# First layer of batches 1 to 3 in two levels of the seven-product scheme, with block sums on GpSimd

## The chip, the cores and the metric

The kernel runs on one core of one Trainium2 chip. The metric is the device time of one execution in microseconds, all work included, from one launch. Lower is better. The core has five engines with queues of their own: PE (matrix products, with PEld for the load of the stationary operand), DVE, ACT, POOL (GpSimd) and SP, which only issues transfers here.

## What is computed

Attention with a bucket mask for 4 batches of 8 heads of 768 x 64, then a Fourier mix, a normalisation and a two-layer network. Cut to what matters:

```python
# q, k, v: (4, 8, 768, 64); proj: (64, 6)
mask = bucket(q @ proj)[..., :, None] == bucket(k @ proj)[..., None, :]
attn = softmax(where(mask, q @ k.T / 8, -1e9))
x = heads_side_by_side(attn @ v)                      # (4, 768, 512)

mixed = real(fft(fft(x, axis=1), axis=2))
u = x + mixed
un = (u - mean(u)) / sqrt(var(u) + 1e-6)
out = u + maximum(un @ w_ch1, 0) @ w_ch2              # w_ch1: 512 x 2048, w_ch2: 2048 x 512
```

All products are in float32. The change is in `un @ w_ch1`, the first layer.

## The kernel before, in words

**Stages.** After the attention of all batches, each batch goes through `mix(b)`: the Fourier products (lines 1071 and 1100), with DVE adding the results to x (line 1114), and then `mlp7(b)`, the two layers. The 2048 rows of the first layer's output are worked in two halves: first layer half 0, second layer half 0 (`outer7`), first layer half 1, second layer half 1. The second layer's matmuls are at line 1275, the first layer's at line 1394.

**Seven products.** Both layers use Winograd's form of Strassen's scheme: a product of two matrices cut in 2 x 2 blocks is made of seven block products instead of eight, with sums of blocks ahead of and behind them. In the first layer the weights are the left matrix, 16 block rows of 128; for each of eight pairs of block rows `f` (four in a half) there are seven products (`A11, S2, A12, S1, S3, S4, A22`), each of two matmuls, 128 x 128 on 128 x 384. The left sums are made once, in batch 0, by `quarters(f)` (line 1181), and are written to DRAM (`ad`, lines 1193 and 1194). Batches 1 to 3 read the left blocks back through a ring of 12 slots of 128 KB that lies where the weights w1 were (`fetch`, line 1367, on SP's queue); one block is fetched for each product. The right sums (t1 to t4 of 768 columns, lines 1372 to 1379) are made of x by DVE at the start of the batch.

**Evictions.** ACT copies a product from PSUM, DVE adds the copies in SBUF, ACT applies relu (lines 1434 to 1463). The result `hall` has four blocks c11, c12, c21, c22, each 4 x 384 columns in a half.

**Around it.** `across` (line 1121) turns x by PE (four transposes a tile of 128 rows, line 1126), and ACT copies the result out for the second layer; in batches 1 to 3 three of six tiles are turned ahead of the products and three after the first `f`. `spread` (line 1129) makes each row's scale, with two operations on POOL (lines 1136, 1137). `fold(b + 1)` (line 959) is DVE work for the next batch. In batch 0 `weights2` (line 1213) brings the second layer's weights, fetched on POOL's queue (line 714) and converted by ACT and DVE in turn with the first layer; its sums end at line 1244. `store` sends results from POOL's queue (line 947; SP's in the last batch). In the mix POOL sets a few columns of F to zero (line 1062).

**The range test.** `guard` (line 1487) reads q and k again in 32 pieces of 384 KB and lets ACT sum their squares, in turn with batches 1 and 2. It has three slots (`nq`) and fetches two pieces ahead from POOL's queue (line 1497); the square is at line 1508.

**Order.** In this part of the kernel the code gives an order by its generators, and instructions of each engine can be moved ahead of others where their operands allow; `in_turn` and `issue_after` hold some of them behind named instructions. On the chip each queue is then worked strictly in its order.

Of the kernel before, what the change touches and what calls it, by code (L numbers as in the profile page):

```python
# [20 lines left out]
P = 128  # L21
# [462 lines left out]
def _main(  # L484
# [39 lines left out]
    def pt(shape, name):  # L524
        return banks[0](shape, name)
# [639 lines left out]
    ]  # L1165
    at = NR * 2 * P
# [7 lines left out]
    side = [w1f[:, at + i * HALF : at + (i + 1) * HALF] for i in range(2)]  # L1174
# [163 lines left out]
    def mlp7(b):  # L1338
# [6 lines left out]
        ut, sd, ss = [*us], side, s1s  # L1345
        if b == 0:
# [10 lines left out]
            sd = [s1s[0].rearrange("p r n -> p (r n)")[:, 0:HALF]] * 2  # L1357
            ss = [s1s[0], spare[3].rearrange("p (r n) -> p r n", n=P)]
        prods = [A11, S2, A12, S1, S3, S4, A22]
        right = {A11: b11, S2: t2, A12: b21, S1: t1, S3: t3, S4: b22, A22: t4}  # L1360
        todo = [(f, i) for f in range(HF) for i in prods]
        fetched = [0]

        def fetch():
            n = fetched[0]
            if b and n < len(todo):
                nc.sync.dma_start(ring[n % NR], ad[todo[n][0], todo[n][1]])
                fetched[0] += 1

        for _ in range(NR):  # L1370
            fetch()
        nc.vector.tensor_tensor(t1, b12, b11, op=ALU.subtract)
        nc.vector.tensor_tensor(t2, b22, t1, op=ALU.subtract)
        nc.vector.tensor_tensor(t4, b21, t2, op=ALU.subtract)
# [3 lines left out]
        rs = {}  # L1378
        nc.vector.tensor_tensor(t3, b22, b12, op=ALU.subtract)
        hall = late.tile([P, 2, HF // 2, S], F32, tag="F", name=f"h{b}")  # L1380
        done = [0]

        def product(i, ps, start=True):
            n = done[0]
            left = ring[n % NR]
            if b == 0:
                f = n // 7
                if i >= S2:
                    left = qs[:, f % 2, i - S2].rearrange("p (k m) -> p k m", m=P)
                else:  # L1390
                    c, r = (0 if i == A11 else 2), (f + HF if i == A22 else f)
                    left = w1[:, c : c + 2, r * P : (r + 1) * P]
# [6 lines left out]
            fetch()  # L1399
# [3 lines left out]
        def relu(h):  # L1403

            if b == 0:
                held.append(h)
            else:
                done_by[ET.Activation] = nc.scalar.activation(h, h, AF.Relu)  # L1408

        def behind_copy(ins):  # L1410

            if ins is not None and b == 0:
                done_by[ET.Activation] = ins
# [5 lines left out]
        def inner(half):  # L1419
            for r in range(HF // 2):  # L1420
# [28 lines left out]
                nc.scalar.copy(sd[0], p7)  # L1449
                nc.vector.tensor_tensor(c22, c22, sd[0], op=ALU.add)  # L1450
# [10 lines left out]
                behind_copy(nc.scalar.copy(sd[1], p7))  # L1461
                done_by[ET.DVE] = nc.vector.tensor_tensor(c21, c21, sd[1], op=ALU.add)
                relu(c21)
                if b == 0 and f < HF - 1:
                    quarters(f + 1)
# [4 lines left out]

        for half in range(2):
# [8 lines left out]
            for _ in outer7(b, half, hall, ut, rs, ss):  # L1480
                next(ahead, None)
                yield
            for _ in ahead:
                pass


    def guard():

        nq = {}

        def fetch(i):
            if i < 2 * NPAIR * B:
                n, io = divmod(i, 2)
                b, t = divmod(n, NPAIR)
                tl = late.tile([P, S], F32, tag="nq", name=f"nq{i}", bufs=3)
                s = (k if io else q)[b, 2 * t : 2 * t + 2].rearrange("h s d -> (h s d)")
                nc.gpsimd.dma_start(tl, s.rearrange("(p c) -> p c", p=P))
                nq[i] = tl

        with in_turn():  # L1500
            fetch(0)
            fetch(1)
        yield
        for i in range(2 * NPAIR * B):
            with in_turn():
                fetch(i + 2)
                junk = late.tile([P, S], BF16, tag="junk", name=f"junk{i}")
# [97 lines left out]
```

## Time and profile before

| what | us |
|---|---|
| median of 3 runs | 1014.23 |
| lowest, highest | 1014.07, 1014.61 |
| the profiled execution | 1013.47 |
| its span | 1011.7 |

How to read the profile: busy times of PE overlap between instructions, so the rate of matmuls is read from start to start. A matmul of the code in float32 is two records in the trace. In a row of the timeline "x4" means four merged instructions of that kind, and the second number is from the first one's start to the last one's end. In a row of a window the numbers after the length are the busy times of PE, PEld, DVE, ACT and POOL with their instruction counts, the granted clock, the share of the transfer engines and GB/s; a window of one line has only the engines that the line uses.

### The profile page before, as it was taken

The page shows a single profiled execution, that of the slowest core. Times are in us where ns is not written, and L with a number is a line of the kernel's source. Part 1 is how long each engine was busy: PE and PEld are TensorE (multiplying, and loading weights), DVE is VectorE, ACT ScalarE, POOL GpSimd, SP SyncE. Part 2 cuts the span into 40 slices and gives each one's busy share as a digit, 9 for nine tenths or more (in the row PEclk, how much of TensorE's full clock was granted, in tenths as well). Part 3 has the DMA queues.
Part 4 walks back from the last instruction along what each step waited for, and adds up shares of the span by engine and source line. Part 5 has one row for each costly group of instructions (what it writes and reads, how often), then busy time and mean ns, then how long its engine had stood idle before and what let it go on. Part 6 is the DMA issues. An engine that isn't in the chain of part 4 may idle for free.

```text
span 1011.7 us, 14410 instructions
## 1 busy us (share of the span) xinstructions
PE 998.4 (99%) x5169; PEld 651.4 (64%) x5169; DVE 674.0 (67%) x1198; ACT 512.3 (51%) x1029; POOL 87.2 (9%) x179
## 2 busy tenths in 40 slices
PE   8999999999999999999999999999999999999997
PEld 5444444444444766866885785897686689678576
DVE  4788898878986698579979543549553445454353
ACT  5787887878766566066046515234623402531520
POOL 3000000000000101100214100121200020200000
PEclk9999999999999999999999999999999999999999
DMA  9645363554610438036345543154516223314201
GB/s 142 125 90 112 86 160 56 118 98 98 131 41 13 135 105 293 9 99 245 107 170 173 170 161 104 53 198 125 162 58 195 86 87 122 94 53 143 86 21 45
DMA packets 174880, 115.61 MB, mean 114 GB/s; under 512 B 126672, under 2 KB 159952, under 8 KB 174800
## 3 DMA queue, kind: packets, MB, share of 16 engines
q1 hardware_dynamic: 166224, 88.12, 32.4%
q0 software_dynamic: 7008, 26.09, 8.3%
q8 instruction: 43, 0.70, 0.3%
q10 hardware_dynamic: 1568, 0.39, 0.2%
q14 instruction: 37, 0.30, 0.1%
HBM read 93.59 MB, written 20.97 MB: 113 GB/s over the span
## 4 chain that ended last, share of the span: by engine, by line
PE 90%; DVE 5%; ACT 2%; DMA 2%; issue 1%; POOL 1%; SPq 0%; DVEq 0%; ACTq 0%; POOLq 0%
PE o L1275 29%; PE h_p L1394 22%; PE oo L875 13%; PE sc L858 12%; PE sc L848 4%; PE cs L1071 3%; PE A L1100 2%; PE B L1100 2%; PE sum L895 1%; PE bits L812 1%; DMA zraw<-in_moe_w_ch_dram 1%; PE un L1126 1%; DMA kn<-in_k_dram 1%; DVE bs L1132 0%; DMA pjr<-in_proj_dram 0%
## 5 line engine op out<-in xcount | busy, mean ns | idle before, releaser
L1275 PE MATMUL o<-w,h 128*128 128x256 f32 x1152 | 253.9, 379 | 0.0
L1275 PEld LDWEIGHTS o<-w,h 128*128 128x128 f32 x1152 | 219.1, 190 | 30.9
L865 ACT ACTIVATE pk<-sc 128x768 f32<-128x768 f32 x192 | 152.5, 813 | 34.9 <-PE sc L858 31.4
L1394 PE MATMUL h_p<-x,w 128*128 128x384 f32 x448 | 160.7, 488 | 1.9 <-ACT h L1434 1.8
L858 PE MATMUL sc<-qt,kt 64*128 64x384 f32 x768 | 155.6, 482 | 0.0
L875 PE MATMUL oo<-pk,vn 128*64 128x385 f32 (+1 forms) x768 | 134.4, 492 | 0.0
L1394 PEld LDWEIGHTS h_p<-x,w 128*128 128x128 f32 x448 | 84.0, 190 | 60.9 <-ACT h L1434 6.6
L932 DVE TENSOR_TENSOR acc<-acc,pk 128x1536 f32<-128x1536 f32 x63 | 110.1, 1747 | 3.1
L1394 PE MATMUL h_p<-w 128*128 128x384 f32 x288 | 104.8, 486 | 0.0
L875 PEld LDWEIGHTS oo<-pk,vn 128*64 128x64 f32 x768 | 50.9, 136 | 81.0 <-issue 79.2
L858 PEld LDWEIGHTS sc<-qt,kt 64*128 64x128 f32 x768 | 69.5, 188 | 30.5 <-issue 30.0
L1394 PEld LDWEIGHTS h_p<-w 128*128 128x128 f32 x288 | 54.5, 190 | 37.4 <-PE un L1126 0.4
L1287 DVE SCALAR_TENSOR_TENSOR w<-o,rs,w 128x256 f32<-128x256 f32 x56 | 26.9, 481 | 70.4 <-PE o L1275 69.6
L1305 ACT COPY tq<-o 128x256 f32<-128x256 f32 x24 | 8.9, 372 | 105.4 <-PE o L1275 105.4
L1408 ACT ACTIVATE h<-h 128x384 f32<-128x384 f32 x72 | 37.8, 524 | 32.4 <-DVE h L1450 13.4
L848 PEld LDWEIGHTS <-kk 33*128 33x128 bf16 x384 | 19.7, 93 | 50.8 <-issue 28.0
L1294 ACT COPY tq<-o 128x256 f32<-128x256 f32 x24 | 8.9, 369 | 72.0 <-PE o L1275 72.0
L1445 DVE TENSOR_TENSOR h<-h 128x384 f32<-128x384 f32 x32 | 17.8, 556 | 38.2 <-ACT h L1444 38.1
L1275 PE MATMUL o<-w 128*128 128x256 f32 x176 | 41.6, 379 | 0.0
L1321 DVE TENSOR_TENSOR tq<-tq,o 128x256 f32<-128x256 f32 x24 | 10.1, 419 | 40.4 <-PE o L1275 40.4
L1275 PEld LDWEIGHTS o<-w 128*128 128x128 f32 x176 | 33.5, 190 | 4.5
L1438 DVE TENSOR_TENSOR h<-h 128x384 f32<-128x384 f32 x32 | 17.8, 556 | 27.6 <-ACT h L1437 27.4
(162 smaller groups left out, 1370.8 us busy)
## 6 DMA issues: line engine op xcount, KB each, us to landing
w<-ad SPq DMA_DIRECT2D x168, 128.0 KB, 2.1
w<-bd SPq DMA_DIRECT2D x42, 512.0 KB, 4.6
zraw<-in_moe_w_ch_dram SPq DMA_DIRECT2D x16, 512.0 KB, 4.5
zraw<-in_moe_w_ch_dram POOLq DMA_DIRECT2D x16, 512.0 KB, 4.3
bd<-w SPq DMA_DIRECT2D x14, 512.0 KB, 3.5
vn<-in_v_dram SPq DMA_DIRECT2D x32, 192.0 KB, 3.1
nq<-in_q_dram POOLq DMA_DIRECT2D x16, 384.0 KB, 3.7
nq<-in_k_dram POOLq DMA_DIRECT2D x16, 384.0 KB, 3.8
```

Source lines behind the costliest of these rows:

```text
L848: nc.tensor.matmul(pss[g][:, h, 0:HALF], kk[r, ks], bits[1][r] if g else bits[0][r, h], start=start, stop=not start,)
L858: nc.tensor.matmul(pss[g][:, h, 0:HALF], kt[rows, ks], qt[rows, g * HALF : (g + 1) * HALF], start=early, stop=not early,)
L865: nc.scalar.activation(pk[:, g, :, 0:HALF], pss[g][:, :, 0:HALF], AF.Exp, scale=SCALE)
L875: nc.tensor.matmul(oos[g][h * D : (h + 1) * D, 0:w], nat["v", n][:, (2 * c + h) * D : (2 * c + h + 1) * D], pk[:, g, h, 0:w], start=(c == ...
L932: nc.vector.tensor_tensor(acc, (first[:, :, :, 0:HALF] if c == 1 else acc), new, op=ALU.add)
L1071: nc.tensor.matmul(ps[:, pc + 2 * lo : pc + 2 * hi - 1 : 2], z[:, cp, pc, par, t * P : (t + 1) * P], ch[:, cp, pc, lo:hi], start=(cp == 0) ...
L1100: nc.tensor.matmul(ps[:, cols], F[:, par, k, t, j * P : (j + 1) * P], sq[:, t, k, cols], start=(t == 0), stop=(t == 1),)
L1275: nc.tensor.matmul(ps, a[:, r], right7[i][:, r], start=start and r == 0, stop=r == HF // 2 - 1, skip_group_check=not start,)
L1287: nc.vector.scalar_tensor_tensor(t[:, cols], src, r, t[:, cols], op0=ALU.mult, op1=ALU.add)
L1394: nc.tensor.matmul(ps, left[:, k], right[i][:, k], start=start and k == 0, stop=k == 1, skip_group_check=not start,)
L1408: done_by[ET.Activation] = nc.scalar.activation(h, h, AF.Relu)
L1438: done_by[ET.DVE] = nc.vector.tensor_tensor(c21, c12, c21, op=ALU.add)
```

## The change

In batches 1 to 3 each of the seven products of the first layer is itself split into seven. Two block rows of the left side are taken together (`f` and `f + 2` of a half), the right side of 384 columns in two of 192, and each of the 7 x 7 leaf products of a half is two matmuls, 128 x 128 on 128 x 192. That is 98 leaf products a batch where there were 56 products, each still with one left block of 128 KB from DRAM.

- **Left sums.** `blocks2(half)`, run beside batch 0's second layer, reads each of the seven left blocks of a half (512 KB), makes four sums of 512 columns on GpSimd and writes 512 KB to a new DRAM tensor `ad2`, on SP's queue.
- **Right sums.** At the start of a batch `two_levels` makes the four first-level sums on DVE, then `divided` makes four second-level sums of 384 columns for each product: for A11, S2 and A12 on DVE, for S1, S3, A22 and S4 on GpSimd. Some are written over x, so all six tiles of `across` stand ahead of them.
- **Order of leaves.** A product's leaves are seven numbers of a key `7 n + 2 j`, so that two products are interleaved. Each product has four banks.
- **Evictions.** ACT copies two leaves of seven, DVE adds five from PSUM. S4's leaves are added straight onto c12's blocks. Five 1536-column sums a half that join the products (`behind`) are on GpSimd, one on DVE; q0 (the second layer's `tq`) and q1 hold two products each in turn.
- **Range test.** One slot, `side`; the square is written over it, and the next piece is fetched from ACT's queue behind the square.

Batch 0 keeps the one-level form. The loop over the halves is now a function `halves`, which pulls `blocks2` at every second step of batch 0's second layer. The core of the diff:

```diff
+    ad2 = tc.dram_tile([2, 7, 4, P, 2, P], F32, name="ad2")
+    def blocks2(half):
+        rows = slice(half * HF // 2, (half + 1) * HF // 2)
+        both_ = late.tile([P, 2, 2, 8 * P], F32, tag="r2", name=f"blocks{half}")
+        for i in range(7):
+            src = both_[:, i % 2, 0].rearrange("p (f k m) -> p f k m", k=2, m=P)
+            dst = both_[:, i % 2, 1].rearrange("p (s g m) -> p s g m", g=2, m=P)
+            nc.sync.dma_start(src, ad[rows, i].rearrange("f p k m -> p f k m"))
...
+            nc.gpsimd.tensor_tensor(s1, lc, ld, op=ALU.add)
+            nc.gpsimd.tensor_tensor(s2, s1, la, op=ALU.subtract)
+            nc.gpsimd.tensor_tensor(s3, la, lc, op=ALU.subtract)
+            nc.gpsimd.tensor_tensor(s4, lb, s2, op=ALU.subtract)
+            nc.sync.dma_start(ad2[half, i].rearrange("s p g m -> p s g m"), dst)
+            yield
...
-                if b and f == 0:
-                    for T in range(3):
-                        across(b, T, ut[T])
...
-            for _ in outer7(b, half, hall, ut, rs, ss):
+            second = blocks2(half) if b == 0 else iter(())
+            for i, _ in enumerate(outer7(b, half, hall, ut, rs, ss)):
                 next(ahead, None)
+                if i % 2 == 0:
+                    next(second, None)
                 yield
...
+    def two_levels(b, right, hall, ut):
+        order = [A11, S2, A12, S1, S3, A22, S4]
+        leaves = sorted(
+            (half, 7 * n + 2 * j, i, leaf)
+            for half in range(2)
+            for n, i in enumerate(order)
+            for j, leaf in enumerate(range(7))
+        )
...
+        def divided(eng, i):
...
+            for d, x, y in ((t1, rb, ra), (t2, rd, t1), (t4, rc, t2), (rb, rd, rb)):
+                eng.tensor_tensor(d, x, y, op=ALU.subtract)
+            parts[i] = ra, t2, t1, rc, rb, rd, t4
+        for T in range(NT):
+            across(b, T, ut[T])
+        V, G = nc.vector, nc.gpsimd
+        V.tensor_tensor(right[S1], right[S3], right[A11], op=ALU.subtract)
+        V.tensor_tensor(right[S2], right[S4], right[S1], op=ALU.subtract)
+        divided(V, A11)
+        V.tensor_tensor(right[A22], right[A12], right[S2], op=ALU.subtract)
+        V.tensor_tensor(right[S3], right[S4], right[S3], op=ALU.subtract)
+        divided(V, S2)
+        divided(V, A12)
+        for i in (S1, S3, A22, S4):
+            divided(G, i)
...
+        to = {A11: c12, S2: q0, A12: q1, S1: c22, S3: q0, A22: q1}
...
+        def placed(i, j, ps):
+            y = to[i]
+            y00, y01, y10, y11 = (block(y, a, c) for a in range(2) for c in range(2))
+            if j == 0:
+                copy(y01, ps[0])
+            elif j == 1:
+                add(y10, y01, ps[1])
+            elif j == 2:
+                add(y11, y10, ps[2])
+            elif j == 3:
+                copy(y00, ps[0])
+            elif j == 4:
+                add(y11, y11, ps[3])
+            elif j == 5:
+                add(y01, y10, ps[2])
+            else:
+                add(y10, y10, ps[3])
...
+        def behind(i):
+            if i == S2:
+                add(c21, c12, q0, G)
+            elif i == A12:
+                add(c11, c12, q1, G)
+                relu(c11)
+            elif i == S1:
+                add(c12, c21, c22, G)
+            elif i == S3:
+                add(c21, c21, q0)
+                add(c22, c22, c21, G)
+                relu(c22)
+            elif i == A22:
+                for n in range(2):
+                    y, x = (t[:, :, n * HH : (n + 1) * HH] for t in (c21, q1))
+                    add(y, y, x, G)
+                    relu(y)
...
+            at = (0, 1, 2, 0, 3, 2, 3)[j]
+            start = at not in ps
+            if start:
+                ps[at] = pt([P, 2, HH], f"h{b}_{half}_{i}_{at}")
+            for g in range(2):
+                nc.tensor.matmul(
+                    ps[at][:, g], ring[n % NR][:, g], parts[i][j],
+                    start=start and g == 0, stop=g == 1, skip_group_check=True,
+                )
+            fetch()
...
     def guard():
...
-                nc.gpsimd.dma_start(tl, s.rearrange("(p c) -> p c", p=P))
+                nc.scalar.dma_start(side, s.rearrange("(p c) -> p c", p=P))
...
                 nc.scalar.activation(
-                    junk, nq.pop(i), AF.Square,
+                    side, side, AF.Square,
                     accum_out=norms[:, i % 2, i // 2 : i // 2 + 1],
                 )
+                fetch(i + 1)
```

More of the change, by code (lines that the diff above doesn't have):

```diff
@@ L1173, in _main @@
     at += 4 * DM
-    side = [w1f[:, at + i * HALF : at + (i + 1) * HALF] for i in range(2)]
+    side = w1f[:, at : at + S]
     HD = DM // 2
@@ L1344, in mlp7 @@
         t3 = b12
-        ut, sd, ss = [*us], side, s1s
+        ut, ss = [*us], s1s
         if b == 0:
```

152 lines of the change are left out of this document (109 added, 43 removed).

## The prediction

> **What bounds the kernel now.** I read the page first (busy shares, then the chain that ended last), then the table of windows cut at the stages, then the timeline inside batch 1.
>
> ```profile
> PE 998.4 (99%) x5169; PEld 651.4 (64%) x5169; DVE 674.0 (67%) x1198; ACT 512.3 (51%) x1029; POOL 87.2 (9%) x179
> PE 90%; DVE 5%; ACT 2%; DMA 2%; issue 1%; POOL 1%; SPq 0%; DVEq 0%; ACTq 0%; POOLq 0%
> 397.00:433.30 36.30, 36.30 (x171) 32.00 (x169) 21.39 (x48) 5.09 (x13) 6.50 (x12) 1.00 0.23 89
> 433.30:471.10 37.80, 37.19 (x114) 20.90 (x113) 32.95 (x79) 31.22 (x69) 3.26 (x6) 1.00 0.54 169
> 471.10:507.30 36.20, 36.20 (x169) 31.93 (x168) 32.81 (x74) 4.76 (x12) 6.98 (x13) 1.00 0.45 147
> 507.30:514.40 7.10, 7.10 (x50) 6.66 (x50) 2.73 (x6) 3.71 (x12) 1.73 (x4) 1.00 0.96 368
> 524.90:564.70 39.80, 36.82 (x112) 20.98 (x112) 1.00 0.48 146
> 601.00:637.10 36.10, 36.10 (x112) 21.08 (x111) 1.00 0.41 126
> 857.20:896.10 38.90, 36.67 (x112) 20.92 (x112) 1.00 0.29 89
> 932.30:968.50 36.20, 36.20 (x112) 21.11 (x111) 1.00 0.30 91
> ```
>
> PE is the bound, almost everywhere without a gap. The first four window rows hold all instructions of batch 0's second layer half 0, first layer half 1, second layer half 1, and the next fold; their columns after the length are PE, PEld, DVE, ACT, POOL, granted clock, DMA share, GB/s. The last four are L1394 alone (PE, PEld, clock, DMA), the two first-layer halves of batch 1 and of batch 3: 224 matmul records a batch, two for each matmul of the code.
>
> **The PE side of the change.**
>
> ```profile
> 538.37 1.45 PE L1394 MATMUL h_p<-w 128*128 128x384 f32 x4
> 539.66 1.45 PE L1394 MATMUL h_p<-x,w 128*128 128x384 f32 x4
> ...
> 522.25 0.82 PE L1100 MATMUL A<-sq,F 128*128 128x193 f32 x4
> 522.90 0.82 PE L1100 MATMUL B<-sq,F 128*128 128x193 f32 x4
> 523.56 0.81 PE L1100 MATMUL A<-sq,F 128*128 128x192 f32 x4
> 524.21 0.81 PE L1100 MATMUL B<-sq,F 128*128 128x192 f32 x4
> 524.86 0.27 PE L1126 MATMUL un<-ident,x 128*128 128x128 f32 x1
> L1100 PEld LDWEIGHTS A<-sq,F 128*128 128x128 f32 x128 | 21.4, 190 | 0.2
> ```
>
> Start to start, four records of 384 columns take 1.29 us, 323 ns each; sixteen of 192 or 193 columns take 2.61 us, 163 ns each, each with a fresh weight load. The load's 190 ns do not show, as loads overlap. So the removed work is 224 x 0.323 = 72.4 us a batch, and the added 2 halves x 49 leaf products x 2 matmuls x 2 records = 392 x 0.163 = 63.9 us. That is 8.5 us less for each of batches 1 to 3. One leaf is 4 x 0.163 = 0.652 us, one half 49 x 0.652 = 31.9 us. What of it arrives depends on the waits below.
>
> **The start of a batch.** All 24 transposes now stand first, since the sums overwrite x. DVE then has two sums of 768 columns, four of 384 (product A11), two of 768, eight of 384, all ahead of the first eviction in its queue.
>
> ```profile
> 534.47 1.47 PE L1126 MATMUL un<-ident,x 128*128 128x128 f32 x12
> 535.78 1.14 PE L1394 MATMUL h_p<-w 128*128 128x384 f32 x3
> ...
> 521.52 0.95 DVE L1372 TENSOR_TENSOR w<-x 128x768 f32<-128x768 f32 x1
> 525.34 1.01 DVE L1114 TENSOR_TENSOR x<-x,B 128x384 f32<-128x384 f32 x2
> 527.41 0.95 DVE L1379 TENSOR_TENSOR x<-x 128x768 f32<-128x768 f32 x1
> 528.28 0.95 DVE L1374 TENSOR_TENSOR w<-x,w 128x768 f32<-128x768 f32 x1
> L932 DVE TENSOR_TENSOR acc<-acc,pk 128x1536 f32<-128x1536 f32 x63 | 110.1, 1747 | 3.1
> ```
>
> I count from the first transpose at 524.86. Twelve transposes take 1.31 us, so 24 take 2.6. The last update of x ends at 526.35, 1.5 in. The first 768-wide sum is early already (521.52); the others step by 0.87 (527.41 to 528.28), those of 384 by 0.51 (two in 1.01). DVE is free at 1.5 + 3 x 0.87 + 12 x 0.51 = 10.2, and has evicted two leaves at 11.2. PE can run the transposes and about ten leaves of two interleaved products on eight banks: 2.6 + 6.5 = 9.1. So PE loses 2.1 us here. After that DVE has, a half, 38 adds of 0.51 and one of 1.75, 21 us of 31.9: it keeps up, but for a burst (the 1536-wide add, then four adds for S4's second leaf) just ahead of the end; with leaf 49 waiting on it I put 0.7 us a half.
>
> Half 0 is then 2.6 + 31.9 + 2.1 + 0.7 = 37.3 against 39.8 (38.9 in batch 3), half 1 31.9 + 0.7 = 32.6 against 36.1. Batches 1, 2: -6.0 each (batch 2 has batch 1's lengths); batch 3: 1.6 + 3.6 = -5.2. Together **-17.2 us**, if GpSimd is in time.
>
> **GpSimd, whose sums no row shows.**
>
> ```profile
> L619 POOL MEMSET kk<- 128x768 bf16 x2 | 1.5, 742 | 0.0
> L620 POOL MEMSET q<- 128x384 bf16 x2 | 0.8, 414 | 0.0
> 540.34 0.22 POOL L1136 TENSOR_SCALAR rs<-mv 128x1 f32<-128x1 f32 x1
> ...
> 543.46 0.55 DVE L1445 TENSOR_TENSOR h<-h 128x384 f32<-128x384 f32 x1
> 543.72 0.95 POOL L1136 TENSOR_SCALAR rs<-mv 128x1 f32<-128x1 f32 x1
> 543.92 0.62 DVE L986 TENSOR_TENSOR z<-ef 128x190 f32<-128x190 f32 x2
> 544.46 0.17 DVE L990 COPY z<-ef 128x4 f32<-128x4 f32 x1
> ```
>
> The memsets give 0.854 ns a column over 86 ns: a floor. Two inputs read one after the other make 1.71, with the write on top 2.56; I take the middle, 2.13: 0.9 us for 384, 1.18 for 512, 3.4 for 1536 columns, and keep 0.854 and 2.56 as ends. [...]
>
> The other rows show a wait. L1136 takes 0.22 us when free, but 0.95 while DVE runs three sums with both inputs in SBUF without a gap; it ends only when the one-input copy has come. So DVE's chain at the start holds GpSimd back. Of the 16 leaf sums on GpSimd in half 0 I let five run ahead of the chain (S1's and S4's first, beside DVE's adds from PSUM) and eleven after 10.2: done at 20.1. Then c21 = c12 + q0 until 23.5. S3's first copy into q0 wants that; PE has its leaf at 21.7 and stops only at S3's fourth leaf, at 25.6: 2 us to spare. c11 follows until 26.9, c12 until 30.3, DVE's c21 until 32.0, c22 until 35.4, the two of c21 until 39.2, its relu until about 40. PE ends its leaves at 37.3, and the second layer has two products of 1.7 us before it needs c21, at 40.7. It just fits. Half 1 has no leaf sums, and room. Cost taken: 0.
>
> **Batch 0.** Here 56 adds of 512 columns (66 us of GpSimd) run beside the second layer, with 28 transfers of 512 KB. Windows 1 to 3 leave DVE 14.9 + 4.9 + 3.4 = 23 us idle. If a GpSimd sum that is under way holds a DVE sum, it costs 1.18 less the one-input DVE work beside it (0.5): 0.7, for about three in four (the rest of DVE's work reads PSUM): 56 x 0.53 = 30, less 23 idle: **+7 us**. The ends are 0 (GpSimd alone waits) and 56 x 1.18 - 23 = +43. [...]
>
> ```profile
> 460.86 0.53 POOL L714 DMA_DIRECT2D zraw<-in_moe_w_ch_dram  x1 [2.81 <-ACT zraw L663]
> 473.32 0.42 DVE L1244 TENSOR_TENSOR w<-w 128x256 f32<-128x256 f32 x1
> 471.08 4.26 PE L1275 MATMUL o<-w,h 128*128 128x256 f32 x19
> ```
>
> The weight fetches on GpSimd's queue stand behind half 0's sums, and the last converted block is ready (473.32) 2.2 us after PE has begun on that half, so a fetch delayed past this cover would delay PE. The stores and the memset of F stand behind half 1's sums; the 7 has room for a part of that only.
>
> **Transfers and the range test.**
>
> ```profile
> w<-ad SPq DMA_DIRECT2D x168, 128.0 KB, 2.1
> L1367 SPq DMA_DIRECT2D w<-ad x168: 319/320/1075, 344.7 to 953.1; - x168
> nq<-in_k_dram POOLq DMA_DIRECT2D x16, 384.0 KB, 3.8
> L1508 ACT ACTIVATE junk<-nq 128x768 bf16<-128x768 f32 x32 | 27.1, 848 | 3.7 <-DMA nq<-in_q_dram 2.1 <-DMA nq<-in_k_dram 1.4
> ```
>
> A leaf fetch of 128 KB each 0.652 us is 201 GB/s; the fold's window moved 368. SP spends 0.32 us on an issue; twelve slots are 7.8 us ahead, landing takes 2.1. So nothing: uncovered, each late leaf would cost PE its lateness. In the range test one slot takes the place of three, and the fetch moves from GpSimd to ACT's queue behind each square. A fetch and its square (3.8 + 0.85) fit the 5.2 us between two turns in the first layer, not quite the 3.5 in the mix (17.6 us, 507.3 to 524.9, for ten steps), where evictions queued behind the square wait about 1 us and PE has spare banks. Nothing, at most 1 us each for four turns in two batches.
>
> **Sum.** The profiled execution took 1013.47 us (span 1011.7): 1013.5 - 17.2 + 7 = 1003.3; the median shown, 1014.23, is 0.8 higher. **1004 us.**
>
> **Rivals.** *GpSimd is no obstacle* (994 to 997, chance 0.24): batch 0 costs nothing, as when GpSimd alone waits; 1014.2 - 17.2 = 997, less some of the 2.1 at each start if other leaves fill it. For it: GpSimd is 9% busy. Against: DVE is without a gap in most of window 3.
> *GpSimd late in half 0* (1016, chance 0.2): at 2.56 ns, or with all 16 leaf sums behind DVE's chain (4.5 us later), c21's relu ends near 44.5, and PE waits some 4 us: 3 x 4 = 12 on 1004. For it: only 0.7 us to spare.
> *Batch 0's sums hold DVE* (slower; about 1025, chance 0.16): the mechanism of the +7 at a greater price; with 0.9 us held for each, 56 x 0.9 - 23 = 27. It decides for slower from (17.2 + 23) / 56 = 0.72 us for each. For it: window 3's DVE at 32.8 of 36.2. Against: DVE's long unbroken runs keep GpSimd out.
> *The leaves don't run at 163 ns* (1028, chance 0.04): at the load's 190 ns, 392 x 0.19 = 74.5, more than 72.4; L1100 speaks against it.
> My forecast (998 to 1009) has 0.36.
>
> **How the numbers follow.** About 0.2%, 2 us, is what a measurement of this kernel tells from no change. Forecast and first rival are faster (0.60); of the late-GpSimd case (1009 to 1019) 0.02 is faster, 0.09 the same, 0.09 slower; the others are slower (0.20). The range takes the first rival's middle at one end and the batch-0 case's middle at the other: 990 to 1025, leaving out about 0.18.
>
> **What would show it.** Leaf matmuls 163 ns apart, 392 a batch; half 1 about 32.6 us, half 0 about 37; PE's gap at each start ended by DVE; GpSimd's 512-column sum 1.0 to 1.4 us, longer beside two-input DVE sums; batch 0's second-layer half 1 longer than 36.2 with DVE sums lengthened. It would be wrong if GpSimd's waits reach PE in half 1 too, if leaf fetches come late, or if PE gaps in batch 0 pass 20 us.

## The result and the profile after

| | before | after |
|---|---|---|
| median, us | 1014.15 | 1079.37 |
| profiled execution, its span | 1013.5, 1011.7 | 1078.7, 1077.0 |
| mean granted clock of TensorE | 0.998 | 0.975 |
| batch 0: transposes and both layers | 151.2 | 176.2 |
| mix before batch 1 | 17.5 | 18.7 |
| batch 1, 2, 3: transposes and both layers | 148.5, 148.8, 147.7 | 161.6, 164.6, 157.1 |

The changed kernel takes 1.063 times as long (95% interval 1.060 to 1.066), 65 us more, where 10 less was forecast. One of its four executions took 1453.3 us at a granted clock of 0.654; the ratio is that of the other three, whose median is 1078.7 us. A batch is counted from the start of its first transpose (`un`) on PE to that of the next mix's first product (`cs`), batch 3 to the end of its last product, read from the timeline. The rows that differ add up: 25.0 + 1.2 + 13.1 + 15.8 + 9.4 = 64.5 us.

The page of the changed kernel, the two lines that were shown of before:

```profile
PE 1001.4 (93%) x5673; PEld 731.6 (68%) x5673; DVE 807.7 (75%) x1354; ACT 477.8 (44%) x915; POOL 250.0 (23%) x287
PE 69%; DVE 16%; DMA 5%; issue 4%; POOL 3%; ACT 2%; SPq 0%; DVEq 0%; ACTq 0%; POOLq 0%
```

PE's share of the chain that ended last fell from 90% to 69%; what came in is DVE, 5% to 16%. PE is still the busiest engine, but it now waits. The windows of the same stages follow: all instructions of batch 0's second layer half 0, first layer half 1 and second layer half 1, then the leaf products alone (PE, PEld, clock, DMA share, GB/s) of both first-layer halves of batch 1 and of batch 3.

```profile
403.20:451.20 48.00, 38.59 (x170) 32.92 (x169) 26.20 (x57) 6.54 (x16) 20.79 (x33) 0.93 0.66 228
451.20:489.20 38.00, 37.31 (x114) 20.91 (x113) 33.99 (x79) 31.51 (x70) 6.36 (x10) 1.00 0.52 163
489.20:531.70 42.50, 36.92 (x171) 31.64 (x170) 39.30 (x76) 4.56 (x12) 18.01 (x27) 1.00 0.71 236
...
550.40:603.20 52.80, 35.37 (x196) 33.33 (x196) 0.97 0.57 171
637.40:676.30 38.90, 33.57 (x196) 32.59 (x194) 0.93 0.66 194
911.50:959.60 48.10, 36.25 (x196) 34.33 (x196) 0.91 0.45 132
995.30:1033.50 38.20, 32.88 (x196) 32.12 (x194) 0.96 0.53 156
```

The second layer's half 0 of batch 0 is 48.0 us where it was 36.3, half 1 42.5 where it was 36.2. Another 7.3 us of batch 0's 25 lie ahead of these windows, in its transposes and first layer half 0 (355.1 to 403.2, 48.1 us, where the same took 40.8 before). In batches 1 and 3 the leaf windows reach from the first transpose to the last leaf, with early second-layer products in between; PE is busy with leaves 33 to 36 us of them, near the forecast 31.9, and the clock is below 1 in all four. The timeline shows why (columns: start, busy, engine, line, operation, output<-input, and in brackets the idle time before with its releaser):

```profile
343.14 0.73 POOL L1181 TENSOR_TENSOR blocks<-blocks 128x256 f32<-128x256 f32 x1 [11.97 <-DMA blocks<-ad]
...
348.86 1.16 POOL L714 DMA_DIRECT2D zraw<-in_moe_w_ch_dram  x2
...
354.21 0.43 DVE L643 TENSOR_SCALAR w<-zraw 128x512 int32<-128x512 int32 x1 [5.36 <-DMA zraw<-in_moe_w_ch_dram]
...
358.47 0.33 PE L1126 MATMUL un<-ident,x 128*128 128x128 f32 x1 [3.02 <-DVE x L1114]
...
413.83 0.71 POOL L1181 TENSOR_TENSOR blocks<-blocks 128x256 f32<-128x256 f32 x1 [10.51 <-DMA blocks<-ad]
...
415.31 0.23 POOL L1136 TENSOR_SCALAR rs<-mv 128x1 f32<-128x1 f32 x1
...
418.57 0.48 DVE L1309 SCALAR_TENSOR_TENSOR w<-o,rs,w 128x256 f32<-128x256 f32 x1 [7.76 <-POOL rs L1137]
...
421.45 0.77 PE L1297 MATMUL o<-w,h 128*128 128x256 f32 x1 [7.74 <-DVE mv L1134]
...
569.72 3.43 POOL L1570 TENSOR_TENSOR h<-h,tq 128x1536 f32<-128x1536 f32 x1 [0.81 <-DVE mv L1134]
...
570.16 3.40 DVE L976 TENSOR_TENSOR ef<-ef 128x384 f32<-128x384 f32 x1
...
576.63 3.68 POOL L1570 TENSOR_TENSOR h<-h,sum 128x1536 f32<-128x1536 f32 x1 [1.39 <-DVE sum L1570]
...
576.95 3.39 DVE L990 COPY z<-ef 128x4 f32<-128x4 f32 x1
...
917.38 0.74 DVE L1537 TENSOR_TENSOR sums<-x 128x192 f32<-128x192 f32 x1
...
917.87 0.70 POOL L1537 TENSOR_TENSOR sums<-x,sums 128x192 f32<-128x192 f32 x1
918.04 0.74 DVE L1537 TENSOR_TENSOR sums<-w,sums 128x192 f32<-128x192 f32 x1
918.53 0.70 POOL L1537 TENSOR_TENSOR x<-x 128x192 f32<-128x192 f32 x1
...
923.67 1.65 PE L1647 MATMUL h<-x,w 128*128 128x192 f32 x4 [2.93 <-DVE h L1570]
...
947.01 0.81 PE L1647 MATMUL h<-w 128*128 128x192 f32 x4
947.66 1.63 PE L1647 MATMUL h<-sums,w 128*128 128x192 f32 x8
...
947.91 3.44 POOL L1570 TENSOR_TENSOR h<-h 128x1536 f32<-128x1536 f32 x1 [1.87 <-DVE h L1570]
...
949.39 4.93 DVE L1570 TENSOR_TENSOR h<-h,tq 128x384 f32<-128x384 f32 x3
...
951.43 2.01 POOL L1570 TENSOR_TENSOR h<-h,sum 128x768 f32<-128x768 f32 x1
...
954.84 1.65 PE L1647 MATMUL h<-x,w 128*128 128x192 f32 x4 [3.82 <-DVE h L1570]
```

Four readings.

- *Batch 0 (343 to 359, 413 to 421).* The block sums do not only run beside the second layer: the first stands at the head of GpSimd's queue from 331 us on, ahead of the first mix, and waits 12.0 us for its load. Two weight fetches are behind it; VectorE stands 5.4 us for their data with updates of x behind that, and PE waits 3.0 us at its transposes. At 413 GpSimd stands 10.5 us at another block sum whose load has not landed. The `rs` of the normalisation is behind it in its queue, VectorE waits 7.8 us for `rs`, PE 7.7 for VectorE.
- *The fold in batch 1 (569 to 580).* Two VectorE instructions last until a 1536-column sum on GpSimd is over: a sum of 384 columns takes 3.40 us and ends 0.4 us after it, and a copy of four columns, which took 0.17 before, takes 3.39 and ends with it.
- *The start of batch 3 (917 to 923).* VectorE's leaf sums and GpSimd's take turns one for one: a VectorE sum of 192 columns comes every 0.66 us (917.38 to 918.04), and PE waits 2.9 us for the eviction behind them.
- *The end of a half (947 to 955).* The three adds of S4's second leaf take 4.93 us together, while GpSimd does a sum of 3.44 and one of 2.01; PE waits 3.8. The four leaf records after that wait take 1.65 us, where four take 0.81 at 947.01: half the rate.

### The profile page after: what moved, and what is told of

It reads as the page before. It is cut to its first block, busy times and chain, and to the rows that moved or that the text cites. A ratio compares the mean times of both kernels' runs of the same rounds, so it can differ in the third digit from the quotient of the medians.

```text
span 1077.0 us, 16146 instructions
## 1 busy us (share of the span) xinstructions
PE 1001.4 (93%) x5673; PEld 731.6 (68%) x5673; DVE 807.7 (75%) x1354; ACT 477.8 (44%) x915; POOL 250.0 (23%) x287
## 4 chain that ended last, share of the span: by engine, by line
PE 69%; DVE 16%; DMA 5%; issue 4%; POOL 3%; ACT 2%; SPq 0%; DVEq 0%; ACTq 0%; POOLq 0%
PE o L1297 22%; PE oo L875 12%; PE h L1647 11%; PE sc L858 11%; DVE h L1570 4%; PE sc L848 3%; PE h_p L1408 3%; PE cs L1071 1%; DVE sums L1537 1%; DMA zraw<-in_moe_w_ch_dram 1%; PE sum L895 1%; PE A L1100 1%; DMA blocks<-ad 1%; POOL h L1570 1%; PE bits L812 1%
## 5 line engine op out<-in xcount | busy, mean ns | idle before, releaser
L1647 PE MATMUL h<-sums,w 128*128 128x192 f32 x504 | 101.9, 338 | 12.1 <-DVE h L1570 6.3
L1647 PE MATMUL h<-x,w 128*128 128x192 f32 x384 | 85.7, 350 | 26.6 <-DVE h L1570 26.4
L1647 PEld LDWEIGHTS h<-sums,w 128*128 128x128 f32 x504 | 88.1, 198 | 15.1 <-DVE h L1570 6.9
L1647 PEld LDWEIGHTS h<-x,w 128*128 128x128 f32 x384 | 69.5, 204 | 31.0 <-DVE h L1570 29.7
L1309 DVE SCALAR_TENSOR_TENSOR w<-o,rs,w 128x256 f32<-128x256 f32 x56 | 26.9, 480 | 66.0 <-PE o L1297 58.1
L1570 DVE TENSOR_TENSOR h<-h,h 128x384 f32<-128x384 f32 x90 | 48.5, 547 | 21.0 <-PE h L1647 19.8
L1567 ACT ACTIVATE h<-h 128x384 f32<-128x384 f32 (+2 forms) x48 | 39.0, 839 | 52.4 <-POOL h L1570 44.5
L1647 PE MATMUL h<-w 128*128 128x192 f32 x288 | 60.5, 332 | 0.0
L1570 POOL TENSOR_TENSOR h<-h,tq 128x1536 f32<-128x1536 f32 x6 | 20.7, 3446 | 151.0 <-DVE tq L1570 147.3
L1647 PEld LDWEIGHTS h<-w 128*128 128x128 f32 x288 | 50.6, 196 | 0.0
L1570 POOL TENSOR_TENSOR h<-h,sum 128x768 f32<-128x768 f32 (+1 forms) x18 | 44.7, 2487 | 17.2 <-DVE sum L1570 16.3
```

The lines of the kernel that those rows point to most:

```text
L1309: nc.vector.scalar_tensor_tensor(t[:, cols], src, r, t[:, cols], op0=ALU.mult, op1=ALU.add)
L1567: done_by[ET.Activation] = nc.scalar.activation(d, d, AF.Relu)
L1570: ins = eng.tensor_tensor(d, x, y, op=ALU.add)
L1647: nc.tensor.matmul(ps[at][:, g], ring[n % NR][:, g], parts[i][j], start=start and g == 0, stop=g == 1, skip_group_check=True,)
```

## The experiments

Line numbers in the expectations and edits are those of the changed kernel; in the rows of a kernel they are its own. Times are medians, of two executions in the first two parts and of four to ten in the third; before was between 1014.2 and 1015.3 beside each of them. Times of batches are those of the one profiled execution.

### What batch 0 pays

**No block sums.** `second = iter(())`, and the S leaves read `ad[half * HF // 2 + j, i]`.

> The changed kernel without blocks2: no loads of the stored first-level quarters, no block sums, no second-level stores; the second-level S leaves read the stored first-level blocks instead, so the number and size of leaf fetches stay. Left out: the second-level sums of the left side. It bounds what batch 0 pays for blocks2 by any way. In the changed kernel's trace batch 0's MLP (from the first transpose to the next mix) is 176.2 us against 151.2 before, the mix after it 1.2 longer. If blocks2 is the cause (queue, lock or traffic alike): the MLP of batch 0 back to about 151, in all 1079.4 - 26 = 1053 us, batches 1 to 3 unchanged (162, 164, 157). If batch 0 pays for something else of the change (the range test on ScalarE's queue, the clock): above 1070.

Measured: 1055.1 us, batch 0 151.5, batches 1 to 3 164.8, 162.7, 157.4. So the whole loss of batch 0 comes from `blocks2`; the mix stays at 18.5, so its 1 us doesn't come from there.

**Loads and stores without the sums.**

> blocks2 keeps its loads and stores (28 transfers of 512 KB), its four GpSimd sums of each step are taken out; what was loaded is stored. Left out: the sums themselves. Theory (GpSimd's instructions are the cost: they stand in GpSimd's queue ahead of the rs of the normalisation and the weight fetches, waiting for their load, and hold shared access against VectorE): as the kernel without blocks2, 1053 us, batch 0's MLP near 151. Rival (the transfers, SyncE's queue or the DMA share are the cost): 1070 to 1079, MLP near 170.

Measured: 1057.1 us, batch 0 153.8. In batch 0 the 28 transfers cost about 2 us (no more than the two executions differ by), GpSimd's 56 sums the other 22, by their work or by what waits behind them.

**The `rs` ahead of the sums.**

```diff
+            with tc.issue_after(last_pow):
                 nc.gpsimd.tensor_tensor(s1, lc, ld, op=ALU.add)
```

> All block sums stay, but each is queued on GpSimd behind the last rs of the normalisation traced before it, so that the mix's weight fetches and each tile's rs go out ahead of sums that wait for a load. Nothing is left out. Theory (a queue: sums that wait for their load block what stands behind them): the waits at the transposes (4.6 us) and at the second layer's half 0 (7.7 with the lowered clock, 11.8 in all) go, the second layer's half 1 (42.7) keeps what the sums do to VectorE there: 1079.4 - 6 - 10 = 1063 us, 1059 to 1067. Rival (shared access: while GpSimd adds, VectorE's sums take twice the time, wherever the sums stand): the sums only move, half 1 of the second layer grows by what half 0 gains: 1073 to 1082.

Measured: 1075.6 us, so the theory fell by the number. The stages say otherwise: transposes and second layer half 0 were back (36.4 us), but the first layer's half 1 took 52.2 (38.0). The rival's sign did not show either: the second layer's half 1, which it expected to grow, took 42.4. The timeline of the first layer's half 1:

```profile
442.50 0.81 POOL L1191 TENSOR_TENSOR blocks<-blocks 128x256 f32<-128x256 f32 x1 [7.21 <-DMA blocks<-ad]
...
454.02 1.19 POOL L723 DMA_DIRECT2D zraw<-in_moe_w_ch_dram  x2
...
459.39 0.43 DVE L643 TENSOR_SCALAR w<-zraw 128x512 int32<-128x512 int32 x1 [10.37 <-DMA zraw<-in_moe_w_ch_dram]
...
461.89 1.65 PE L1418 MATMUL h_p<-x,qs 128*128 128x384 f32 x2 [12.45 <-ACT h L1464]
```

The queue's wait had moved: now the weight fetches stood behind sums that waited for their loads, and PE waited 12.5 us in the end.

**All sums behind the last weight fetch.** `second = chain(blocks2(0), blocks2(1))` in half 1 alone, each sum behind the last `rs` and fetch.

> All 56 block sums stay on GpSimd, but stand behind the last rs and behind the last weight fetch of batch 0's second half: they run in the second layer's half 1 of batch 0 and in the mix after it. Nothing is left out. In the run before this one, with each tile's rs first, the transposes and the second layer's half 0 fell back to 36.4 us, but the first layer's half 1 grew from 38 to 52 us: there the weight fetches stood behind sums that waited 7.2 us for their load. Theory (the queue is the larger part of batch 0's loss, shared access the smaller): with nothing behind the sums but stores, transposes, half 0 and the first layer's half 1 are back (about -18), half 1 of the second layer keeps its 6 and the mix or batch 1's start may lose up to 8: 1061 us, 1059 to 1069. Rival (shared access alone, the sums cost the same wherever they stand): 1074 to 1082, with the second layer's half 1 near 60 us.

Measured: 1091.8 us, a miss on both sides. Batch 0 did fall to 165.3, but the sums ran on until 567 us, over 20 us into batch 1. The `rs` of batch 1 were now behind them in GpSimd's queue, and VectorE stood 13.1 us for these, 10.5 of them at once. The leaf sums behind that in VectorE's queue take the memory of the blocks and waited for their last store, 0.65 us more; it was issued at 567.2 and would have held them in any case:

```profile
548.52 0.92 PE L1659 MATMUL h<-x,w 128*128 128x192 f32 x4 [1.78 <-ACT h L1576]
...
562.75 0.18 DVE L1145 BATCH_NORM_AGGREGATE mv<-bs 128x2 f32<-128x6 f32 x1 [10.54 <-POOL rs L1147]
...
570.21 0.36 DVE L1549 TENSOR_TENSOR sums<-x 128x192 f32<-128x192 f32 x1 [0.65 <-DMA ad<-blocks]
...
571.21 2.90 PE L1659 MATMUL h<-sums,w 128*128 128x192 f32 x8 [21.77 <-issue]
...
571.29 0.35 DVE L1549 TENSOR_TENSOR sums<-x,sums 128x192 f32<-128x192 f32 x1
...
571.49 0.60 POOL L1549 TENSOR_TENSOR sums<-w 128x192 f32<-128x192 f32 x1
571.56 0.75 DVE L1549 TENSOR_TENSOR sums<-w,sums 128x192 f32<-128x192 f32 x1
```

Together the two runs show that what is queued behind a waiting sum is late wherever the sum stands, and that in neither of the two places did GpSimd do the 56 sums with their waits unnoticed. The last rows show the sharing at its onset: VectorE's sum of 192 columns takes 0.35 us, and 0.75 from the sum at which GpSimd begins its own.

**The block sums on VectorE.** `nc.gpsimd` becomes `nc.vector` in `blocks2`, behind an update of x.

> The 56 block sums are done by VectorE in place of GpSimd, each step queued behind an update of x that is traced after its load. Nothing is left out, batches 1 to 3 stay as in the changed kernel. 56 sums of 256 columns at 0.34 us a step are 19 us of VectorE, which was idle 23 us in batch 0 before. Theory (what GpSimd's sums cost is the queue and the mutual exclusion, not the work itself): batch 0's MLP between 151 and 160, in all 1055 to 1064, likeliest 1058. Rival (VectorE has no room there, and its own queue then waits for the loads): batch 0's MLP at 170 or more, 1073 and up.

Measured: 1058.3 us, as the theory had it; batch 0 155.6. The mix before batch 1 took 22.4, with PE waiting 3.0 us for ScalarE, which stood 3.1 us at a square of the range test whose fetch was late.

### What batches 1 to 3 pay

**Every sum of the batches on VectorE.** `V = G = nc.vector`.

> In batches 1 to 3 every sum that the change gives to GpSimd (16 leaf sums of 192 columns a batch, and in each half three sums of 1536 columns, one more of 1536 into c22, two of 768) is given to VectorE; nothing is left out, batch 0 stays as it is. Theory (VectorE and GpSimd exclude each other, so GpSimd's sums cost VectorE their whole time and more): VectorE does them in 16 x 0.34 and 5 x 1.75 us a half instead of waiting for 16 x 0.7 and 5 x 3.45: the start of a batch stays about as long (4.8 + 16 x 0.3 = 9.6 against 9.1), the tail of each half shrinks from 3.8 us of PE's wait with a lowered clock behind it to about 1: 1079.4 - 6 x 3 = 1061, between 1050 and 1075. Rival (VectorE's queue is simply too long, and GpSimd takes work off it): VectorE gets 16 x 0.3 + 2 x 5 x 1.75 = 22 us more a batch: 1090 to 1140.

Measured: 1035.1 us, 44 faster than the changed kernel, better than the range of the theory; batches 145.7, 146.9, 144.9. VectorE has more to do and PE waits less. The groups of instructions show the price of sharing (busy us, mean ns of one | idle before). In the changed kernel these are GpSimd's block sums that wait for a load (batch 0), S4's second leaf on VectorE, and PE's waits for VectorE's adds (us in total, times, longest):

```profile
L1181 POOL TENSOR_TENSOR blocks<-blocks 128x256 f32<-128x256 f32 x14 | 11.0, 785 | 58.1 <-DMA blocks<-ad 58.1
...
L1570 DVE TENSOR_TENSOR h<-h,tq 128x384 f32<-128x384 f32 x18 | 29.0, 1662 | 0.0
...
PE h L1647 <- DVE h L1570: 32.7, 11, 3.8
```

then S4's second leaf and the same waits with every sum of the batches on VectorE:

```profile
L1570 DVE TENSOR_TENSOR h<-h,tq 128x384 f32<-128x384 f32 x18 | 9.0, 556 | 0.0
...
PE h L1647 <- DVE h L1570: 0.2, 1, 0.2
```

The same eighteen adds take a third of the time, and PE hardly waits for VectorE's adds.

**Only the leaf sums on VectorE**, `divided(V, i)`:

> Half of the run in which VectorE does all sums of batches 1 to 3 (1035.1 us): only the 16 leaf sums of 192 columns a batch go to VectorE, the sums of 1536 columns stay on GpSimd. Nothing is left out. Theory (mutual exclusion at the start): the start's wait of PE (2.9 us and a halved clock after it) goes, as VectorE's sums alone take 0.34 and not 0.74: 4 to 6 us a batch, 1079.4 - 15 = 1064, 1060 to 1068; the waits at the ends of the halves stay. Rival (the start is bound by the number of sums ahead of the first eviction): VectorE's chain gets 16 x 0.34 = 5.4 longer, and each batch loses 0 to 5 us: 1079 to 1094.

Measured: 1064.7 us; batches 157.9, 155.0, 155.1.

**Only the product sums on VectorE**, the `G` of `behind` taken out:

> The other half: the leaf sums stay on GpSimd, the sums of the seven products (five of 1536 columns, one of them in two halves, in each half) go to VectorE. Nothing is left out. Theory (mutual exclusion at the ends of the halves and in the fold): VectorE's two-input sums are no longer stretched from 0.5 to 1.7 us at S4's second leaf, nor the fold's from 0.55 to 3.4: six halves win 3.5 and the clock after it, two batches another 3 to 5: 1079.4 - 30 = 1049, 1044 to 1056. Rival (VectorE has too little room for 5 x 1.75 = 8.8 us more a half): the tails grow, 1075 to 1100.

Measured: 1044.8 us; batches 147.7, 149.4, 147.6. From 1078.7 us the two halves give 14.0 and 34.0 us, 48 together, where both at once gave 44: they overlap a little, if at all, as the changed kernel's own executions differ by 4 us. With the leaf sums on VectorE PE's waits of 2.6 to 2.9 us for VectorE's adds at the starts are gone and those at the ends stay; with the product sums there it is the other way round, and the waits in the fold are gone too. So leaf sums cost the starts, product sums the ends and the fold.

**The adds of S4 from PSUM, GpSimd's sums left as they are.**

```diff
-            if j == 0:
-                copy(u, ps[0])
-            elif j == 1:
-                add(u, u, ps[1])
+            if j < 2:
                 for y in (y11, y10, y01):
-                    add(y, y, u)
+                    add(y, y, ps[j])
```

> GpSimd keeps all its sums. Only S4's first two leaves change: each is added to its three blocks of c12 from its PSUM bank (six adds with one input in SBUF) in place of one copy, one add from PSUM and three adds with both inputs in SBUF. Nothing is left out. Theory (at the ends of the halves VectorE's two-SBUF adds wait for GpSimd's sums into c22 and c21, which run beside them; adds from PSUM don't take part in the exclusion): the adds take 0.55 us each again, PE's waits of 3.5 to 3.8 us there shrink to about 1 although VectorE has two more instructions: six halves by 2.5 and the clock after it, 1079.4 - 18 = 1061, 1054 to 1068. Rival (PE waits there because GpSimd's sums themselves come late, or VectorE's queue is too long): no gain or a loss, 1077 to 1085.

Measured: 1057.3 us, as the theory had it. GpSimd still adds beside them, and in each of six halves six adds from PSUM have taken the place of one from PSUM and three within SBUF; the group grows from 90 by 36, at its usual length (547 ns in the changed kernel):

```profile
L1570 DVE TENSOR_TENSOR h<-h,h 128x384 f32<-128x384 f32 x126 | 66.1, 546 | 17.0 <-PE h L1643 15.5
```

PE's waits at the six ends, 2.1 to 3.8 us in the changed kernel, are 1.7 or less; those at the starts and in the fold stay. So neither a late GpSimd nor a full VectorE makes PE wait at the ends, but what VectorE's adds read. (Three of the adds also come one leaf earlier here, which was not tried apart.) The times say the same in the changed kernel: the eighteen adds of S4's second leaf, with both inputs in SBUF, took 1662 ns on average, while four adds of the same size with one input in PSUM took 0.55 us each beside a GpSimd sum of 3.45 us (942.59 to 946.04). By what means the two engines hold each other is not shown.

### Towards a version that gains

**Everything on VectorE, the second half's block sums in batch 1** (beside its second layer, the fold moved on to half 1, the leaf fetches held until those sums are stored):

> What the runs so far point to, together; nothing is left out. All sums of batches 1 to 3 on VectorE; the block sums on VectorE too, those of the first half in batch 0's second layer half 0 (where VectorE was idle 14.9 us), those of the second half in batch 1's second layer half 0, with batch 2's fold moved to half 1 of batch 1; the range test starts after batch 1's mix. Batches 1 to 3 at 145.7 + 1, 146.9, 144.9 as in the run with VectorE alone (445.0 before: -6.5), batch 0 at 151.2 + 2, mix after it 17.5: 1014.2 - 6.5 + 2 = 1010 us, 1005 to 1016. By the rival (VectorE has no room for the block sums) batch 0 at 160 and batch 1 at 152: 1025.

Measured: 1034.3 us, above the forecast and the rival's 1025. Batch 1 took 165.4: VectorE stood 7.3 us at block sums behind transfers of the blocks, and PE waited 4.7 us in half 1 for leaf fetches, which had been held until the sums were stored.

**Everything on VectorE, block sums in batch 0, and S4's leaves in another order.** The order is `(0, 1, 4, 3, 6, 2, 5)`; the range test begins at step 11 in place of 2.

> Nothing is left out. Block sums on VectorE in batch 0 as in the run that had them there (batch 0's MLP 155.6, mix 22.4), all sums of batches 1 to 3 on VectorE (145.7, 146.9, 144.9), the range test from batch 1's MLP on, and S4's seven leaves in another order (the two that end the right half of c12's columns last, since the second layer's first tile needs the left half). From the stages of those two runs: against before's 1014.2, batch 0 +4.5, mix +1 (the range test's wait for its slot, 3.2 us in that run, gone from it), batches 1 to 3 -7.5, the order of S4's leaves -1 at each of six ends: 1014.2 + 4.5 + 1 - 7.5 - 6 = 1006 us, 1002 to 1013. Rival (VectorE is so full that block sums and batch sums together find no room, as in the run with the second half's block sums in batch 1): 1020 or more.

Measured: 1018.6 us (ratio 1.0038, interval 1.0023 to 1.0053), between the theory's range and the rival's 1020. Batch 3 now took 142.6, against 147.7 before: 5.1 us less, and 5.2 were forecast for it. Batch 1 took 155.0, with 4.4 us of PE's waits at its transposes.

**The sums written over their blocks**, so that four loads stand ahead of VectorE:

> As the run before it (1018.6 us), but the block sums are written over their own blocks, so that four loads instead of two can stand ahead of VectorE, and those of the second half run mostly after batch 0's last products, in the mix, where VectorE is idle; nothing is left out. In that run batch 1 lost 5.5 us at its transposes, as VectorE's updates of x stood behind block sums that waited 2.9 and 3.1 us for their load, and batches 1 and 2 lost 4.8 to late leaf fetches. Theory (what is left of batch 0's cost is VectorE's queue waiting for loads): the 5.5 go, 1013 us, 1009 to 1016. Rival (VectorE's work itself is what delays the updates of x): 1016 to 1021.

Measured: 1020.0 us, no gain; batch 1 158.0, mix before it 18.4. The fifth load of the second half was the late one, once again with VectorE's updates of x behind it:

```profile
519.65 0.42 DVE L1191 TENSOR_TENSOR blocks<-blocks 128x256 f32<-128x256 f32 x1 [5.60 <-DMA blocks<-ad]
```

**No block sums at all, the rest on VectorE:**

> No block sums at all (the second-level S leaves read the first-level blocks), all sums of batches 1 to 3 on VectorE, S4's leaves in the other order, the range test from batch 1's MLP on. Left out: the second-level sums of the left side. It gives the change without GpSimd and without blocks2. The forecast's own terms: batches 1 and 2 -6.0 each, batch 3 -5.2, so 1014.2 - 17.2 = 997 us if what is left of the loss in batches 1 and 2 comes from the block sums (batch 1 at 143, batch 2 at 143). If it comes from the range test's fetches beside the leaf fetches: batch 1 and 2 stay at 147 to 150 and the whole at 1003 to 1006.

Measured: 1009.5 us, above both numbers; batches 148.2, 149.8, 142.9. With the block sums gone batches 1 and 2 still lack the 6 us forecast and batch 3 has its 5. PE's waits (us in total, times, longest):

```profile
PE o L1297 <- ACT h L1567: 7.8, 6, 2.4
PE h L1647 <- DMA w<-ad: 5.4, 4, 2.9
```

**The second half's blocks of A11, A12 and A22 summed where they stand in SBUF**, no load for them:

> As the run with the sums written over their blocks (1020.0 us), but the second half's blocks of the products A11, A12 and A22 are summed where they stand in SBUF, so that only four of its seven products need a load, and all four loads stand ahead in four slots. Nothing is left out. In that run VectorE stood 5.6 us in the mix before batch 1 waiting for a block's load, and its updates of x behind it cost PE 4.9 us of waits at the transposes and 2.9 us after them. Theory (VectorE's queue behind a load): those 5 to 8 us go, 1013 us, 1010 to 1016. Rival (VectorE's work itself): 1017 to 1021.

Measured: 1013.6 us, ratio 0.9999 (0.9988 to 1.0010); batches 151.1, 151.4, 147.5, 143.0. Batch 1 is 6.6 us shorter than in the run before last, and the mix is back at 17.5, so waits for loads were the larger part of what batch 1's start still paid.

**The range test only beside the second layers, with two slots:**

```diff
-            other = after(11, other, islice(guards, NPAIR * B + 1))
+            other = within(
+                [22, *range(23, 35), *range(48, 60)], other, islice(guards, NPAIR * B + 1)
+            )
```

> As the run with the second half's blocks summed where they stand (1013.6 us; batches 151.1, 151.4, 147.5, 143.0), but the range test of batches 1 and 2 runs only beside their second layers, a step at each turn there, with two slots. Nothing is left out. Theory (its fetches of 384 KB beside the leaf fetches, and its squares ahead of a relu, are what batches 1 and 2 lose against batch 3): the waits for leaf fetches (4.6 us) and 0.7 us at two ends go: 1013.6 - 6 = 1008 us, 1005 to 1011. Rival (the fold on VectorE, or the leaf fetches by themselves): 1012 to 1016; the second layers, where ScalarE evicts three products a tile, could also wait for squares: up to 1020.

Measured: **1007.0 us**, ratio 0.9932 (0.9919 to 0.9946) to before: 0.7% faster than the kernel before. Batches 151.8, 148.4, 144.0, 142.9. Its page:

```profile
PE 977.6 (97%) x5673; PEld 713.3 (71%) x5673; DVE 821.2 (82%) x1494; ACT 478.0 (48%) x915; POOL 68.5 (7%) x147
```

PE is busy 20.8 us less than before (998.4); the forecast's 8.5 a batch would be 25.5. The run changes two things, when the range test runs and its number of slots; they were not tried apart.

## Why the prediction was wrong

The forecast was 1004 us, 75 below what was measured. Two terms carry it: "-17.2 us" for batches 1 to 3, which came out as 13.1 + 15.8 + 9.4 = +38.3, and "+7" for batch 0, which came out as +25 and 1.2 in the mix.

- **The PE side: right.** Four leaf records start 0.65 us after the four before (947.01 to 947.66), 163 ns each, and there are 392 a batch.
- **GpSimd: the step that failed.** It ended in "It just fits" and "Cost taken: 0". Its duration was right where it counts: 1536 columns take 3.44 us, forecast 3.4. But it asked only whether GpSimd's results come in time. The row beside it (L1136, 0.95 in place of 0.22) showed VectorE holding GpSimd back; the other direction was weighed in batch 0 alone, though the same kind of sums ran in the batches. There it decides: with these sums on VectorE the three batches took 437.5 us, in the changed kernel 483.2 (before 445.0). So it cost 46 us, with the slower clock that followed the waits. Without it the batches gained 7.5 of the 17.2 us, and 9.7 in the fastest version.
- **The start of a batch: 2.1 us forecast, 2.9 and a halved clock (0.50) measured**, for another reason than forecast, so the near number is luck. The section on the change and the prediction take the leaf sums for 384 columns wide, a step of 0.51; they are 192, which VectorE alone does in 0.35. In turns with GpSimd each took 0.74, and one started every 0.66.
- **The end of a half: 0.7 us forecast, up to 3.8 measured.** "A burst" of VectorE was seen, GpSimd's sum beside it not. (VectorE has 39 adds of 384 columns a half, not 38; that changes nothing.) One of the prediction's own signs of being wrong came with it: PE waits in half 1 as well, 38.2 us in batch 3 where 32.6 was forecast.
- **Batch 0: +7 forecast, +25 measured.** The term took 512 columns and 1.18 us for each sum; they have 256 and took 0.81 on average. So each sum was priced too high. No run shows the 0.53 us for each that the +7 is made of; in its place the runs showed 22 us for the 56 sums with all that waited behind them, and, for its condition that a GpSimd sum under way holds a VectorE sum, 3.40 us in place of 0.55 for a sum of 384 columns in the fold of batch 1. And a wait was left out: sums that wait for their load at the head of GpSimd's queue (58.1 us of idle time in all), with `rs` and fetches behind, and that from before the first mix on. The prediction did note that the fetches stand behind the sums, but gave this no time of its own, and the loads' none at all. How much of the 25 us is this queue and how much the sharing was not measured apart: the 6 us of the second layer's half 1 go with VectorE busy 39.3 us in place of 32.8 there, as sharing would have it.
- **Range test and fetches: forecast 0, at most 1 us each for four turns.** The mix lost 1.2 as allowed. In batches 1 and 2 it was 3.0 and 3.5 us: 151.4 to 148.4 and 147.5 to 144.0 when it was moved out of the first layers and got a second slot. What it cost in the changed kernel, behind the greater waits there, was not measured.
- **The rivals.** The one in which block sums hold VectorE named the right side and a mechanism that took part, in batch 0 only, at 1025. None had VectorE held in the batches.
- **The clock** was not in the forecast. Of PE's ten waits of 2.6 to 3.8 us for VectorE's adds ahead of leaves, six are followed by leaves at half rate (four records in 1.65 us in place of 0.81); the mean granted clock fell to 0.975, and is 0.997 in the fastest version. How many of the 65 us are the clock's own was not measured apart from the waits; an estimate from the mean clocks and spans sets a ceiling: (1 - 0.975) x 1077.0 less (1 - 0.998) x 1011.7, 25 us.

What stays open: batch 1 of the fastest version gains nothing yet (148.4 against 148.5); PE waits 3.1 us there for updates of x. In VectorE's queue a leaf sum of batch 1 is ahead of these; it takes the memory of the blocks and stands 3.4 us until a store of the blocks has landed (at 523.25). Other memory for the leaf sums was not tried. PE's six waits for a relu at the ends of halves (6.4 us) were left too.

## What to carry to other kernels

Before work goes to an engine that is idle, ask what it shares with the engine that it relieves: in this kernel a VectorE sum of 384 columns with both operands in SBUF took 3.40 us in place of 0.55 beside a GpSimd sum of 1536 columns (3.43), which VectorE itself does in 1.75, while adds with one operand in PSUM kept their 0.55 us beside such a sum. Ask it for both directions and in every stage in which the two run, above all at the ends where PE waits for the last eviction. And in this kernel an instruction that waited for a transfer kept what stood behind it in its queue waiting too, for up to 12.0 us: hold such an instruction back until its data is there, or give it a queue where nothing urgent follows.

## What was not expected of the hardware

- VectorE and GpSimd alternated one for one while both had sums of two SBUF operands queued: at the start of batch 3 a pair of 192-column sums came every 0.66 us, where VectorE alone takes 0.35 for one and GpSimd's quickest is 0.59.
- A VectorE copy of four columns within SBUF, with a single input, waited as long as a sum: 3.39 us in place of 0.17 beside a GpSimd sum of 3.68.
- A wait of 2.9 us was enough for the granted clock to fall: four leaf records took 1.65 us in place of 0.81, and the clock is 0.50 from 923.26 to 926.67, for 3.41 us. A wait of 2.6 us did the same (0.50 from 742.35 to 745.76), while one of 2.7 us, which ended at 494.68, left the clock at 1.00: in the changed kernel a wait of about 3 us may cost the clock or not. What decides it is not shown.
